# A written-out step order exchanged for another one, in an RWKV-6 plus HyperMixer kernel on one core

## The chip, the core and the metric

The kernel runs on one NeuronCore of a Trainium2 chip. The metric is the device time of one execution in microseconds (µs). Three runs of the kernel before took 100.81, 100.89 and 101.01 µs; the median is 100.89 µs.

The profile names the engines PE (matrix multiplies), PEld (the loading of the stationary operand, which overlaps PE), DVE (vector engine), ACT (scalar engine), POOL (GpSimd) and SP, which only issues transfers here. "SPq", "ACTq" and "PEq" are the instruction sequencers of these engines.

## The reference

Inputs are `r, k, v, w` of shape (4 batches, 8 heads, 768 positions, 48), `u` of shape (8, 48) and three small weight matrices. What is computed, cut to its core:

```python
for t in range(S):                       # attention with a decaying state
    y[:, :, t] = r_t · (state + outer(u * k_t, v_t))
    state      = w_t[..., None] * state + outer(k_t, v_t)
x     = y with the heads side by side    # (4, 768, 384)
W_tok = (x @ w_q) (x @ w_k)^T / 8        # a 768 x 768 mixing matrix for each batch
out   = relu(W_tok @ x) @ w_out          # (4, 768, 384), float32
```

## The kernel before, in words

**Tiling.** The 768 positions of a batch are cut into three units of 256 positions; there are 12 units, numbered 0 to 11, so that units 2, 5, 8 and 11 end a batch. A unit is two chunks of 128 positions. Inside a chunk the recurrence is written as matrix products, and a 48 x 48 state per head goes from chunk to chunk.

**Steps.** A unit is a chain of steps with short names, which all texts here use. A number behind a name is the unit (`cw.2` belongs to unit 2), a second one the chunk.
- Loads: `wg`, `kg`, `rg`, `vg` bring a unit's w, k, r and v, 384 KB each, all issued by SP.
- `ln` (ACT, L615) takes the logarithm of w; `cw` (PE) sums it along the positions; `ep` and `en` (ACT, L675 to L686) exponentiate the sums.
- `k16`, `r16`, `v16` (POOL, ACT or DVE, L627 and L800) cast the loads to bf16; `kT`, `rT` (PE) transpose; `vp` (PE) reorders v, and `VB` (ACT or DVE) copies it out of PSUM.
- `ks`, `qT`, `RT` (DVE, some `ks` on ACT) and `KT` (POOL or DVE, L773) make the scaled operands; `A` (PE) multiplies them, `AM` (DVE, L860) masks the product.
- `dps`, `dd`, `Vd` make the diagonal term with `u`; `kb`, `kd`, `sn` (PE), `SB` (DVE, L929) make the new state; `ya`, `yi` (PE) and `X` (DVE, L972) the output y.
- `xt`, `XT`, `wk`, `wq`, `QK` transpose y and project it. At the end of a batch follow `T`, `TS`, `mx`, `rl` (relu, into tile MX), `fp`, `os` and the store `st`.
- `wcast` (POOL, L560 to L562) casts the weights, which the loads `wts` and `wtso` bring. Thirty steps `z` are multiplications of a zero tile that keep PE warm; each one can be issued or left out.

**What sets the order.** Nothing is scheduled at run time. Every engine executes its own list of instructions in the order of the program, and the steps' order in that list is written out by hand-off tables: `RANK` (L243) gives each of 787 steps its place on its engine, `ALT` (L280) says for each step with a choice which way it is done. The letters A, D and P in `ALT` are engines; E and e are two ways of doing a PE step, which use the PE array whole, or in halves by rows, by columns or both (the plan calls these modes 0 to 3, and counts `SWITCH` = 93 ns when the mode changes; f is a third way). E of a `z` step issues it, e leaves it out.

`Plan.order` (L104 to L238) then walks the five lists with a model of time of its own, to fix in which sequence the instructions are written down and which PSUM bank each buffer gets. Its constants stand in L38 to L46: durations, the delay until a result is seen by another engine (`AFTER`), a model of the load queue, and one of the fetching of PE's own instructions: after every `BLOCK` = 128 matmuls, the first time after `FIRST` = 94, the plan lets PE wait until a fetch is done. The time that the plan computes is not carried into the program; only order, ways and banks are.

**Buffers.** Each load has a ring of four buffers (`RINGS`, L361), so a load of unit n waits for the cast of unit n - 4. PSUM has 8 banks, which the plan hands out.

Of the kernel before, what the change touches and what calls it, by code (L numbers as in the profile page):

```python
# [33 lines left out]
class Plan:  # L34
# [1 line left out]


    SWITCH = 93  # L38
    LAND = 1950
    COLD = 5200  # L40
    BLOCK, FIRST = 128, 94
    FETCH = (4700, 3700, 74000)
    DEEP = dict(Q=1850, R=2700, T=1850)
    ASIDE, BLOCKED = 1200, 980
    OVER = dict(A=100, D=80, P=42)
    AFTER = dict(E=200, A=80, D=62, P=65, S=80)  # L46

# [56 lines left out]
    def order(self):  # L104
# [5 lines left out]
        wires = {}  # L110
        for s in self.steps:
            if s["eng"] in "QL":
                wires.setdefault(s["after"][0]["i"], s)
        free = dict.fromkeys("EADPSQRT", 0)
        place = dict.fromkeys("EADPS", 0)
        rings = {k: [] for k in self.rings}
        owners, done, mode, moving = [None] * 8, [], 0, []
        count, edge, ready = 0, self.FIRST, 0
        used = [{} for _ in range(8)]

        def banks(s):
            b = s["banked"]
            if b is None or b.kind == "s" or s["part"] is None:
                return [] if b is None else range(b.bank, b.bank + 1 + (b.kind == "w"))
            return [b.bank + s["part"]]
# [34 lines left out]
                    t = max(t, clear(ring[-size]))  # L160
            return t, None

        def run(s, t, took):
            s["start"], s["end"] = t, t + took + s["lag"]
            free[s["eng"]] = t + took
            done.append(s)
            for x in banks(s):
                used[x][s["eng"]] = s["end"]

        while True:  # L170
            heads = [(start(q[place[e]]), e) for e, q in queues.items() if place[e] < len(q)]
# [4 lines left out]
            s = queues[e][place[e]]  # L176
# [10 lines left out]
            took = s["dur"] + self.SWITCH * change  # L187
            if e == "E" and t < self.COLD and s["fn"] is not None:
                took = took * 8 // 5
            n = s["opts"][s["way"]][5]  # L190
            if n:
                first = count
                count += n
                while count > edge:
                    cross = t + took * (edge - first) // n
                    if cross < ready:
                        took += ready - cross
                        cross = ready
                    ready = cross + self.FETCH[cross >= self.FETCH[2]]
                    held = cross + self.ASIDE  # L200
                    for i, (m, x) in enumerate(moving):
                        if x > held:
                            moving[i][1] = x = x + self.BLOCKED
                            m["end"] = max(m["end"], x)
                            x = wires[m["i"]]
                            x["start"], x["end"] = m["end"], m["end"] + x["dur"]
                    free["R"] = max(free["R"], held) + self.BLOCKED
                    edge += self.BLOCK
            lock = s["lock"] and e == "D"
            if lock:  # L210
                took += max(0, free["P"] - t)
            if s["i"] in wires:
                m = wires[s["i"]]
                x = t + took
                full = [0]
                *durs, deep = m["wires"][s["way"]]
                lanes = [(q, d) for q, d in zip("QRT", durs) if d]
                for q, d in lanes:
                    free[q] = max(free[q], x)
                    full.append(free[q] + deep * d // max(durs[0], 1) - self.DEEP[q])  # L220
                    free[q] += d
                m["start"] = x
                m["end"] = max([x] + [free[q] for q, _ in lanes])
                moving = moving[-3:] + [[m, free["R"]]]
                took = max(took, max(full) - t)
                for q, d in lanes:
                    free[q] = max(free[q], t + took)
                    m["end"] = max(m["end"], t + took)
            run(s, t, took)
            if lock:  # L230
                free["P"] = max(free["P"], t + took)
            if s["i"] in wires:
                done.append(m)
                x = wires[m["i"]]
                x["start"], x["end"] = m["end"], m["end"] + x["dur"]
                done.append(x)
        assert len(done) == len(self.steps)
        return done  # L238

RANK = [  # L243
# [35 lines left out]
]  # L279
ALT = ("DDEDAEAEADPEEEAEDEeEeeAEDPPEDPAeAeDPEefDeEEEEAeAPPEADPeAEAPEeEAEEEeAeDAEAEAeAEAEAEAPAEAD"  # L280
       "PeAEAPEEfAEEEEEAeAAPEDPPeAEAPeEfAEeEEeDEAAPeDPPeDeAPEEEAeEEEDeAAEAEAEAeAEAEAPPEDPPEAEAPE"
       "EfAeeEEeAEDPAEAPPeDEAPEEEAeEEEeDEAPPEDPPeAeDPEeEAEEEEDeAAEAEAeAeAeAEAAPEAPPeAEAPeEEAeEEE"
       "eAeDPPEAPAeAEAPEEEAEEEEeAeAPPEEeDPeAeAPPEEEAEEEeAEDDfDEDADEDeDeeADEAeAeeADeDeAeeDDEeeeEE"
       "eeeEEEeEeeeEeeeEeEeeeEee")

WARM = 30

# [2 lines left out]
def kernel(  # L290
# [13 lines left out]
    B, H, S, D = r.shape  # L304
# [19 lines left out]
    R = C // 2  # L324
# [217 lines left out]
    def weights():  # L542
# [8 lines left out]
        def f_o(e):  # L551
            cuts = (0, C) if e == "S" else (0, FEW, C)
            for p0, p1 in zip(cuts, cuts[1:]):
                nc.sync.dma_start(out=view(wo_f, 0, [[DM, NK], [1, DM]], p0=p0, pn=p1 - p0),
                                  in_=moe_w_out.rearrange("(n p) d -> p n d", p=128)[ds(p0, p1 - p0)])
        l = [plan.dma(("wts",), 1000, 1200, f, deep=1200)[1],
             plan.dma(("wtso",), 500, 1500, f_o, deep=500)[1]]

        def cast(e):
            nc.gpsimd.tensor_scalar_mul(wq_sb, wq_f, scale)  # L560
# [622 lines left out]
```

## Time and profile before

| what | value |
|---|---|
| runs | 100.81, 100.89, 101.01 µs |
| span of the profiled execution (first to last instruction) | 102.1 µs, so 1.2 µs over the median of the runs |
| PE busy | 90.8 µs, 2123 matmuls and as many weight loads |
| DVE, ACT, POOL busy | 82.5, 78.2, 63.0 µs |
| moved by DMA | 24.70 MB, mean 242 GB/s |
| mean granted PE clock | 0.996 of full speed |

The profile has a page for the whole execution and answers questions on it. In its timeline a row gives the start in µs from the first instruction, the time taken, engine, line, operation, the tiles written and read, their shapes, and in brackets how long the engine stood idle before and what ended that. A row "by stretches" gives start and end of a stretch, its length, the busy time of each engine in it with the number of its instructions, the granted clock, the busy share of the DMA engines and the rate in GB/s. A matmul's end is modelled: the matmuls overlap, so the distance from one start to the next says what a step costs.

### The profile page before, as it was taken

Reading aid. Unit: us, or ns where it says so; the run is one execution under the profiler, and the core shown is the slowest. Engines: PE = TensorE matmul, PEld = TensorE weight load, DVE = VectorE, ACT = ScalarE, POOL = GpSimd, SP = SyncE. Lnnn points to the kernel's source line nnn. Section 1 sums busy time; section 2 is a strip of 40 time slices with the busy share of each in tenths; the row PEclk is TensorE's granted clock in tenths of the full one; section 3 lists DMA queues with packets and bytes.
Section 4 is the critical chain, followed back from the end, with each engine's and each line's share of the span. In section 5 each row is a group of like instructions: output and inputs, shape, how many; then the busy total and the mean of one; then the engine's idle time right before and its main releaser. Section 6 shows DMA issues by size and latency. Waiting matters only on the chain.

```text
span 102.1 us, 4927 instructions
## 1 busy us (share of the span) xinstructions
PE 90.8 (89%) x2123; PEld 67.8 (66%) x2123; DVE 82.5 (81%) x154; ACT 78.2 (77%) x137; POOL 63.0 (62%) x76
## 2 busy tenths in 40 slices
PE   5998689997999699899999897979998999999950
PEld 2353456975778596786987885657786869775520
DVE  6319979999999789999998696969898599753560
ACT  5349981999779768799999899795987897558710
POOL 4478687393688947988989859696499304100000
PEclk9999999999999999999999999999999999999998
DMA  1999999999899999999997699910993009140783
GB/s 39 310 323 351 328 332 301 283 317 286 242 325 337 325 257 287 312 307 307 302 281 209 193 277 330 281 37 39 277 336 136 0 37 396 43 157 24 306 310 140
DMA packets 43078, 24.70 MB, mean 242 GB/s; under 512 B 30512, under 2 KB 41904, under 8 KB 43056
## 3 DMA queue, kind: packets, MB, share of 16 engines
q1 hardware_dynamic: 42896, 24.19, 79.5%
q8 instruction: 16, 0.26, 1.0%
q10 hardware_dynamic: 160, 0.20, 0.6%
q14 instruction: 6, 0.05, 0.2%
HBM read 19.66 MB, written 4.72 MB: 239 GB/s over the span
## 4 chain that ended last, share of the span: by engine, by line
PE 64%; DVE 13%; SPq 5%; DMA 5%; issue 5%; POOL 3%; ACT 1%; DVEq 1%; POOLq 0%
PE PS L335 64%; DMA rg<-in_r_dram 5%; DVE AM L860 4%; SPq L395 4%; DVE X L972 4%; POOL KT L773 2%; SPq L401 1%; DVE RT L755 1%; DVE os L521 1%; POOL r L627 1%; DVE SB L929 1%; DVE KT L773 1%; DVE ks L521 1%; DVE qT L744 1%; ACT os L519 0%
## 5 line engine op out<-in xcount | busy, mean ns | idle before, releaser
L860 DVE TENSOR_TENSOR AM<-PS,US 128x1024 bf16<-128x1024 f32 x24 | 29.1, 1216 | 1.8 <-PE PS L335 1.4
L773 POOL TENSOR_TENSOR KT<-ks,en 128x1024 bf16<-128x1024 bf16 x8 | 17.1, 2132 | 8.4 <-DVE ks L521 3.4
L839 POOL TENSOR_TENSOR Vd<-VB,dd 128x768 bf16<-128x768 bf16 (+1 forms) x13 | 17.2, 1328 | 7.3 <-ACT dd L519 5.5
L675 ACT ACTIVATE ep<-PS 128x512 bf16<-128x512 f32 x20 | 11.0, 607 | 4.5 <-PE PS L335 4.5
L335 PE MATMUL PS<-wo,MX 128*64 128x384 bf16 (+1 forms) x102 | 13.8, 328 | 0.0
L972 DVE TENSOR_TENSOR X<-PS,Vd 128x768 bf16<-128x768 f32 (+1 forms) x13 | 11.6, 890 | 2.4 <-PE PS L335 1.9
L335 PEld LDWEIGHTS <-KT 64*128 64x128 bf16 (+3 forms) x360 | 10.1, 97 | 4.6 <-issue 1.9
L686 ACT ACTIVATE en<-PS 128x1024 bf16<-128x1024 f32 (+1 forms) x14 | 12.6, 905 | 0.1
L615 ACT ACTIVATE lw<-wg 128x768 bf16<-128x768 f32 x12 | 10.2, 858 | 2.6 <-DMA wg<-in_w_dram 2.6
L525 ACT ACTIVATE MX<-PS 128x768 bf16<-128x768 f32 (+1 forms) x12 | 8.8, 732 | 2.9 <-PE PS L335 2.8
L519 ACT COPY os<-PS 128x768 f32<-128x768 f32 (+1 forms) x11 | 8.2, 746 | 2.6 <-PE PS L335 2.5
L335 PE MATMUL PS<-RT,KT 64*128 64x128 bf16 (+1 forms) x232 | 9.6, 218 | 0.4 <-ACT XT L517 0.2
L335 PE MATMUL PS<-Z 128*128 128x512 bf16 (+2 forms) x26 | 8.9, 457 | 1.1 <-DVE Z L418 1.0
L335 PE MATMUL PS<-VB,AM 128*128 128x48 bf16 (+1 forms) x200 | 8.2, 184 | 1.3 <-issue 1.3
L335 PEld LDWEIGHTS <-MX 128*64 128x64 bf16 (+1 forms) x102 | 6.8, 104 | 3.6 <-DVE MX L527 0.5
L800 POOL CAST v<-vg 128x768 bf16<-128x768 f32 x9 | 7.5, 828 | 1.9 <-DMA vg<-in_v_dram 1.9
L519 ACT CAST VB<-PS 128x768 bf16<-128x768 f32 x10 | 8.1, 806 | 0.4 <-PE PS L335 0.2
L755 DVE TENSOR_TENSOR RT<-PS,ep 128x512 bf16<-128x512 bf16 x20 | 8.0, 412 | 0.4 <-ACT MX L525 0.4
L744 DVE TENSOR_TENSOR qT<-PS,ks 128x1024 bf16<-128x1024 bf16 x12 | 8.1, 678 | 0.0
L335 PE MATMUL PS<-ID,r 128*128 128x128 bf16 (+1 forms) x120 | 7.2, 213 | 0.9 <-POOL r L627 0.5
L335 PEld LDWEIGHTS <-AM 128*128 128x128 bf16 (+1 forms) x200 | 6.4, 97 | 2.3 <-issue 1.7
L335 PE MATMUL PS<-CM,lw 64*128 64x128 bf16 (+1 forms) x208 | 7.7, 217 | 0.0
(95 smaller groups left out, 195.9 us busy)
## 6 DMA issues: line engine op xcount, KB each, us to landing
wg<-in_w_dram SPq DMA_DIRECT2D x12, 384.0 KB, 5.6
kg<-in_k_dram SPq DMA_DIRECT2D x12, 384.0 KB, 5.3
rg<-in_r_dram SPq DMA_DIRECT2D x12, 384.0 KB, 5.7
vg<-in_v_dram SPq DMA_DIRECT2D x12, 384.0 KB, 6.1
out_dram<-os SPq DMA_DIRECT2D x9, 384.0 KB, 2.9
out_dram<-os SPq DMA_DIRECT2D x5, 192.0 KB, 1.9
wof<-in_moe_w_out_dram SPq DMA_DIRECT2D x1, 576.0 KB
out_dram<-os ACTq DMA_DIRECT2D x1, 192.0 KB
```

Of the source, the lines that this page charges most:

```text
L335: return nc.tensor.matmul(o, l, rr, start=start, stop=stop, skip_group_check=True, is_transpose=trans)
L519: nc.scalar.copy(o, i)
L525: nc.scalar.activation(o, i, ACT.Relu)
L615: nc.scalar.activation(view(lw.tile, 0, [[64, H], [512, 2], [1, D]]), view(g["wg"].tile, 0, [[D2, H], [D, 2], [1, D]]), ACT.Ln, bias=0.0, ...
L675: nc.scalar.activation(view(ep.tile, to, [[EW, 8], [step, 2], [1, Q]]), view(at(cw), x, [[C, 8], [Q, 2], [1, Q]]), ACT.Exp, bias=LIFT, sca ...
L686: nc.scalar.activation(en.tile[:, ds(cs[0] * 512, w_)], at(cw)[:, ds(cs[0] * 512, w_)], ACT.Exp, bias=-LIFT, scale=-1.0)
L744: lambda e: nc.vector.tensor_tensor(plain(qT), turned(second), plain(ks), ALU.mult),
L755: nc.vector.tensor_tensor(view(RT.tile, c * 512, [[256, 2], [Q, 8], [1, Q]]), view(at(kr, BF16), second + c * 256, [[apart, 2], [Q, 8], [1 ...
L773: x.tensor_tensor(KT.tile[:, w], ks.tile[:, w], en.tile[:, w], ALU.mult)
L839: (nc.vector if e == "D" else nc.gpsimd).tensor_tensor(Vd.tile[:, cols], VB.tile[:, cols], view(dd.tile, cs[0] * H, [[1, len(cs) * H], [0, ...
L860: AMs[c] = add(("AM", n, c), {"D": 1221}, lambda e, c=c, A=A: nc.vector.tensor_tensor(view(AM[c].tile, 0, [[C, 8], [1, C]]), view(at(A), 0 ...
L972: lambda e, c0=c0, nc_=nc_: nc.vector.tensor_tensor(view(X.tile, (2 * i + c0) * DM, [[D2, NP * nc_], [D, 2], [1, D]]), view(at(y), c0 * NP ...
```

## The change

No operation of the computation is added or removed. The constants of the plan's model and its treatment of transfers and of instruction fetches are other ones; a transfer now waits in one model queue, a fetch waits for half of what stands before it in that queue and pushes the transfers behind it; and `RANK` and `ALT` are exchanged for tables that were found with that model.

```diff
     SWITCH = 93
-    LAND = 1950
     COLD = 5200
     BLOCK, FIRST = 128, 94
-    FETCH = (4700, 3700, 74000)
-    DEEP = dict(Q=1850, R=2700, T=1850)
-    ASIDE, BLOCKED = 1200, 980
+    ASKED, FETCH, READY = 560, 1000, 1400
+    ARRIVE, AHEAD, LAND, FREE, OPEN = 700, 2600, 450, 220, 2600
+    PATIENT, SLOW = 1300, 1.02
...
-                    ready = cross + self.FETCH[cross >= self.FETCH[2]]
-                    held = cross + self.ASIDE
...
+                    asked = cross + self.ASKED
+                    behind = max(0, free["R"] - asked)
+                    wait = min(behind, (behind + self.PATIENT) // 2)
+                    begin = asked + wait
+                    over = now = begin + self.FETCH
+                    ready = over + self.READY
...
 RANK = [
...
 ALT = (...
...
-             plan.dma(("wtso",), 500, 1500, f_o, deep=500)[1]]
+             plan.dma(("wtso",), 500, 1800, f_o, deep=500)[1]]
```

Read off the tables, the lists differ as follows. Places in the list of SP count from 0.

| list | before | after |
|---|---|---|
| SP, places 3 to 20 | vg.0 wg.1 kg.1 rg.1 vg.1 wg.2 kg.2 rg.2 wg.3 kg.3 rg.3 vg.2 vg.3 wtso wts wg.4 kg.4 rg.4 | rg.1 wg.1 kg.1 vg.0 kg.2 kg.3 vg.1 wg.2 vg.2 rg.2 kg.4 wg.3 rg.3 vg.3 wg.4 wts wtso rg.4 |
| SP, first store | st.2.0 at place 48, among the last loads | st.0.0 at place 38, ahead of 12 loads; then st.2.0 and st.3.0 among the last ones |
| ACT, from `ks.1` on | (another order) | ks.1 ep.1 VB.0 k16.2 VB.1 kd.1 ln.2 v16.2 en.2 ep.2 ln.3 VB.2 en.3 ks.3 ep.3 |
| POOL, from `r16.2` on | r16.2 Vd.1 k16.3 v16.2 v16.3 wcast Vd.2 r16.4 Vd.3 KT.4 | r16.2 k16.4 KT.2 r16.3 v16.3 KT.3 Vd.2 wcast r16.4 KT.4 |
| `KT` | POOL for units 1 and 4 to 10, DVE for 2 and 3 | POOL for units 2 to 10, DVE for 1 |
| PE matmuls | 2123 | 2059 |
| changes of mode along PE's list | 117 | 106 |
| PE, last batch | T.11 fp.7 mx.9 mx.10 fp.8 mx.9 (chunk 1) | fp.7 and fp.8 ahead of T.11; T.11 wq.11 mx.9 mx.10 |

The engines' counts of steps stay near each other: PE 267 and 267, ACT 127 and 124, DVE 138 and 138, POOL 56 and 59.

More of the change, by code (lines that the diff above doesn't have):

```diff
@@ L113, in order @@
                 wires.setdefault(s["after"][0]["i"], s)
-        free = dict.fromkeys("EADPSQRT", 0)
+        free = dict(E=0, A=0, D=0, P=0, S=self.FREE, Q=self.OPEN, R=self.OPEN)
         place = dict.fromkeys("EADPS", 0)
@@ L161, in start, with landed @@
             return t, None
[L163 to L168, printed above, removed]
+        def landed(m):
+            x = wires[m["i"]]
+            x["start"], x["end"] = m["end"], m["end"] + self.LAND
         while True:
@@ L198, in order @@
                         cross = ready
-                    ready = cross + self.FETCH[cross >= self.FETCH[2]]
-                    held = cross + self.ASIDE
[L201 to L207, printed above, removed]
+                    asked = cross + self.ASKED
[4 more added lines that the diff above has]
+                    ready = over + self.READY
+                    for x in moving:
+                        m, b, d = x
+                        if b >= begin - self.PATIENT // 2:
+                            x[1] = max(now, b)
+                            now = x[1] + d
+                            m["end"] = max(m["end"], now)
+                            landed(m)
+                            free["R"] = max(free["R"], now)
+                    free["R"] = max(free["R"], over)
                     edge += self.BLOCK
@@ L213, in order @@
                 m = wires[s["i"]]
[L214 to L229, printed above, removed]
+                d = m["wires"][s["way"]][0]
+                x = t + took + self.ARRIVE
+                q, r = max(free["Q"], x), max(free["R"], x)
+                free["Q"], free["R"] = q + d, r + int(d * self.SLOW)
+                took = max(took, max(q, r) - self.AHEAD - t)
+                m["start"], m["end"] = min(q, r), max(free["Q"], free["R"])
+                moving = moving[-8:] + [[m, r, free["R"] - r]]
+            s["start"], s["end"] = t, t + took + s["lag"]
+            free[e] = t + took
+            done.append(s)
+            for x in banks(s):
+                used[x][e] = s["end"]
             if lock:
@@ L233, in order @@
                 done.append(m)
-                x = wires[m["i"]]
-                x["start"], x["end"] = m["end"], m["end"] + x["dur"]
-                done.append(x)
+                landed(m)
+                done.append(wires[m["i"]])
         assert len(done) == len(self.steps)
@@ L243 @@
 RANK = [
[35 rows of a table removed]
-]
[L280 to L284, printed above, removed]
[35 rows of a table added]
+]
+ALT = ("DDEAPEAEDPDeEEDeDeeEEEDeAAPeADPEAEDPEEfAeEEEEAeDAPeDPAEAEAPEEEDeEEEAeAAEAEAEAEAEAEAPPEAP"
+       "PeAEAPEEfAeEEEEDeAPPEAPAeAEDPEEfDeeEEEAeAAPEAPPeAEDPEEEDEEEeAeDAEAeAEAeAeAEAAPEDPPeAEAPe"
+       "EfAeEEEEDeDPPEAPPeAEAPEEEAEeEEEDeAPPEAPPeAEAPEEEAeEEfAEAAEAeAeAEDEAeAPPEAPPeAEAPeEEDEEEE"
+       "eDEAPPEDPPeAEDPeEEAEEEEeAeAPPEEEDPeAeDPPeEEAEEEEDEDAEAEAADEAeDEEAAeDeAEEDAeAeDEEDDeeeeeE"
+       "eeeeeeEeEeeeeeeEEEEEEeee")
 WARM = 30
```

70 rows, old and new, of the table RANK are left out of this document.

## The prediction, made before the result was known

> **What bounds the kernel now.** I read the page first, then the table by stretches, then PE's waits, and only then single rows of the timeline.
>
> ```profile
> span 102.1 us, 4927 instructions
> ...
> PE 90.8 (89%) x2123; PEld 67.8 (66%) x2123; DVE 82.5 (81%) x154; ACT 78.2 (77%) x137; POOL 63.0 (62%) x76
> ...
> q8 instruction: 16, 0.26, 1.0%
> ```
>
> ```profile
> 20.00:28.00 8.00, 7.25 (x179) 5.80 (x177) 8.00 (x13) 7.23 (x13) 5.33 (x7) 1.00 1.02 283
> ...
> 36.00:56.00 20.00, 19.72 (x502) 16.08 (x502) 19.19 (x30) 18.21 (x33) 16.95 (x15) 1.00 1.00 284
> 56.00:78.00 22.00, 19.79 (x524) 15.57 (x516) 19.10 (x30) 18.56 (x33) 17.09 (x14) 1.00 0.75 219
> ```
>
> Columns are stretch, length, then PE, PEld, DVE, ACT and POOL. From 36 µs on PE is the bound: 19.7 of 20 µs busy, with DVE and ACT close behind. Before that the loads (DMA share 1.0) and, from 20 to 28, DVE (8.00 of 8.00) hold it back. From 56 to 78 PE idles 2.2 µs although nobody else is full. What it waits for:
>
> ```profile
> PE PS L335 <- issue: 3.0, 5, 1.0
> ```
>
> ```profile
> 0.00:29.46 29.46, 25.46 (x477) 1.00 1.00 286
> ...
> 0.00:35.56 35.56, 30.56 (x606) 1.00 1.01 293
> 35.56:56.51 20.95, 20.32 (x512) 1.00 0.98 279
> 56.51:62.16 5.65, 4.90 (x128) 1.00 0.92 263
> 62.16:67.75 5.59, 4.74 (x128) 1.00 0.86 237
> 67.75:77.95 10.20, 9.94 (x256) 1.00 0.63 194
> ```
>
> "Issue" is no semaphore. I cut the span at the ends of these five idle times: 606 matmuls are 94 + 4 x 128, and every further piece holds a whole number of 128. A matmul comes with one weight load, so 128 matmuls are 256 instructions, and 2123 of them make 16 such blocks; the page counts 16 instruction transfers of 16 KB. PE stops where a block of its own program has not come. These five stops cost 3.0 µs. The transfer starts late:
>
> ```profile
> q8 instruction: 1, 0.02, 5.0%
> ```
>
> This is the transfer table for 32.8 to 34.2 µs; PE had entered a new block at 29.46 (the 478th matmul, 94 + 3 x 128) and went on into the next one at 35.57. So in the loaded stretch it takes 6.1, 5.65 and 5.59 µs from entering one block until the next is ready (29.46, 56.51, 62.16). The last stop ends at 77.95; after it, with the loads gone, there is none.
>
> [...]
>
> **The change, term one: PE's own work.** There are 2059 matmuls instead of 2123, and 106 changes of mode instead of 117. A change costs 0.10 µs by the distances between starts:
>
> ```profile
> 38.35 0.40 PE L335 MATMUL PS<-RT,KT 64*128 64x128 bf16 x8
> 38.69 0.36 PE L335 MATMUL PS<-v,PM 64*64 64x384 bf16 x4
> ...
> 41.17 0.40 PE L335 MATMUL PS<-RT,KT 64*128 64x128 bf16 x8 [0.21 <-POOL KT L773]
> 41.41 0.26 PE L335 MATMUL PS<-ID,KT 48*128 48x48 bf16 x8
> ```
>
> (0.34 with a change, 0.24 without.) Eleven fewer give -1.1. Against that, four or five `xt` are done whole instead of in halves:
>
> ```profile
> 25.05 0.35 PE L335 MATMUL PS<-ID,X 64*128 64x64 bf16 x12
> 25.31 0.40 PE L335 MATMUL PS<-RT,KT 64*128 64x128 bf16 x8
> ...
> 27.14 0.50 PE L335 MATMUL PS<-ID,X 128*128 128x128 bf16 x6
> 27.48 0.34 PE L335 MATMUL PS<-UB,qT 128*128 128x2 bf16 x8
> ```
>
> That is 0.34 against 0.26, together +0.4; `vp`, `rT` and `ya` changes add about 0.2. **Term one: -0.5 µs**, bounds -1.1 and 0. Summing every step's distance in this manner, the old list holds 81.4 µs of work without the `z` steps, the new one 80.9; "work" below is this sum up to a step.
>
> **Term two: the stops.** Between block entries the old list has, from the fourth on, 4.7, 5.1, 4.1, 4.7, 6.0, 4.7, 4.6, 4.9, 5.0 µs of work; the new one 5.1, 5.7, 5.3, 5.9, 3.7, 5.2, 5.5, 4.7, 4.2. Against 5.6 to 6.1 until ready, the longer pieces lose less. The short one, 3.7, lies where `st.0.0` stands in SP's list: SP waits there for `os.0`, loads behind it wait too, and the transfer of instructions should meet an empty queue. I take 0.4 for the first piece, 0.5 for the sixth, 0.3 for the rest: 1.2 instead of 3.0. **Term two: -1.8 µs**, bounds -2.8 (only 0.2 left) and +1.0 (6.1 - 5.1, 6.1 - 3.7 and 5.6 - 5.2 all fall due).
>
> **Term three: the front.** Loads arrive in SP's order. Their places and first uses, where the user waited for them:
>
> ```profile
> 4.22 0.84 ACT L615 ACTIVATE lw<-wg 128x768 bf16<-128x768 f32 x1 [2.15 <-DMA wg<-in_w_dram]
> ...
> 11.72 0.83 POOL L627 CAST r<-rg 128x768 bf16<-128x768 f32 x1 [0.31 <-DMA rg<-in_r_dram]
> ...
> 14.16 0.84 ACT L615 ACTIVATE lw<-wg 128x768 bf16<-128x768 f32 x1 [0.45 <-DMA wg<-in_w_dram]
> ...
> 17.65 0.83 POOL L627 CAST r<-rg 128x768 bf16<-128x768 f32 x1 [0.31 <-DMA rg<-in_r_dram]
> ...
> 24.59 0.83 POOL L800 CAST v<-vg 128x768 bf16<-128x768 f32 x1 [1.52 <-DMA vg<-in_v_dram]
> ```
>
> These are places 0, 6, 8, 10 and 15, so a place costs (24.59 - 4.22) / 15 = 1.36 µs. Now `vg.1` moves from place 7 to 9: 16.4. Behind it hang `v16.1` (0.83), `vp.1`, `VB.1` and `kd.1`, and on ACT `ln.2` is queued behind these two.
>
> ```profile
> 13.16 2.13 POOL L773 TENSOR_TENSOR KT<-ks,en 128x1024 bf16<-128x1024 bf16 x1 [0.61 <-DVE ks L521]
> 14.96 0.80 ACT L519 CAST VB<-PS 128x768 bf16<-128x768 f32 x1
> 17.12 0.59 PE L335 MATMUL PS<-CM,lw 64*128 64x128 bf16 x10
> 22.48 1.12 DVE L773 TENSOR_TENSOR KT<-ks,en 128x1024 bf16<-128x1024 bf16 x1
> 25.32 0.68 DVE L773 TENSOR_TENSOR KT<-ks,en 128x1024 bf16<-128x1024 bf16 x1
> 27.45 1.15 POOL L562 CAST wo<-wof 128x1152 bf16<-128x1152 f32 x1
> ```
>
> 16.4 + 0.83 is 17.3; `vp.1` and its way to ACT take 0.5, `VB.1` 0.80, `kd.1` 0.5, `ln.2` 0.84: `cw.2` starts at 20.0 instead of 17.12. The new list does 1.0 µs more work ahead of it, so it is 1.6 behind there. `wg.3` at place 14 comes at 23.2, `cw.3` at 24.1. On POOL follow `KT.2`, `r16.3`, `v16.3` (`vg.3`, place 16, 25.9) and `KT.3`, until 26.7 + 2.13 = 28.8, and PE has `kb.3` behind that; `cw.4` starts at 29.7 with 16.6 of work done, which the old list had done at 28.75. The unit's later loads come earlier than before, and `wcast`, `r16.4` and `KT.4` (2.2 + 0.83 + 2.13 after `Vd.2`) keep up with PE by my count. In return DVE, full from 20 to 28, loses the two `KT` rows, 1.8 µs. **Term three: +0.95**, bounds 0 (DVE's gain pays) and +1.6 (nothing is caught up).
>
> **Term four: the end.** `mx.9` needs `TS.11`, which needs the last `T.11`:
>
> ```profile
> 91.28 0.37 PE L335 MATMUL PS<-X,QK 128*64 128x384 bf16 x2
> ...
> 91.44 1.18 PE L335 MATMUL PS<-wo,MX 128*64 128x384 bf16 x12
> 91.68 0.56 DVE L521 CAST TS<-PS 128x384 bf16<-128x384 f32 x1
> ...
> 92.55 0.36 PEld L335 LDWEIGHTS <-TS 64*128 64x128 bf16 x12 [0.30 <-DVE TS L521]
> ```
>
> From the last `T` to `mx.9` are 1.27 µs, which `fp.7` (91.44) fills. The new list has `fp.7` and `fp.8` earlier, as cover for other waits there, and only 0.46 of work in the hole: 0.8 lost, some 0.3 won elsewhere. **Term four: +0.5**, bounds 0 and +0.8. The output's last steps and stores stay.
>
> The sum is -0.5 - 1.8 + 0.95 + 0.5 = -0.85 on a span of 102.1, so 101.2. The median of the runs lies 1.2 below that span; the forecast for the runs is 100.89 - 0.85, **100.0 µs**.
>
> **Rivals.**
> - *The front costs nothing and the stops go.* For it: DVE, not the loads, was full from 20 to 28. Against it: ACT's queue behind `VB.1`. Terms -0.5, -2.6, +0.2, +0.3: 98.3.
> - *The stop moves to the short block (slower).* If `st.0.0` does not stop the loads while the ninth block is fetched, or its own 384 KB stand before the fetch, the block takes 5.6 to 6.1 against 3.7 of work. It decides from about 4.0 on; the price is 2.0: 102.0. For it: the old list had its worst delays exactly between 50 and 68 µs.
> - *The stops do not come from late instructions*, so all 3.0 stay: -0.5 + 0.95 + 0.5 gives 101.8. Against it: the multiples of 128. [...]
> - *Nothing to measure:* the stops are as long as before at other places, and front and end are covered: about 100.8.
>
> **How the numbers follow.** Forecast 0.45, its own range 99.3 to 100.7; first rival 0.22; the slower one 0.20; late instructions not the cause 0.06; no difference 0.07. A measurement of this kernel tells about 0.2% (0.2 µs) from no change. The forecast's range lies faster for nine tenths of it: faster 0.62, same 0.11, slower 0.27. The range goes from the first rival's 98.3 to the slower one's 102.0.
>
> **What would show it.** Right: PE's "issue" waits near 1.2 µs, none of more than 0.5 between 53 and 58; 2059 matmuls; `cw.2` near 20 and PE idle some 1.8 µs between 15 and 18; `cw.4` near 29.7; an idle 0.8 ahead of `mx.9`. Wrong: issue waits of 3 µs or more, a stop of 2 µs at the ninth block, `cw.4` before 28.8, or a new wait of PE for DVE or POOL between 36 and 78, where I took the old 1.2 µs of other waits unchanged.

## The result, and the profile after

The new lists made the kernel slower. Their runs took 103.85 to 104.97 µs, median 104.64, against a median of 100.95 of the kernel before beside them: a ratio of 1.0325, 95% interval 1.0223 to 1.0428. Two later comparisons, on chips 11 and 5, gave 1.0249 (1.0163 to 1.0336) and 1.0347 (1.024 to 1.0453). Some executions of a kernel are a few per cent slower than the rest (105.49 µs beside 100.81 to 101.01 of the kernel before); the ratios here and below, as recorded, leave those out and are not the quotients of the medians, which are taken over all runs. The forecast was 100.0, the range ended at 102.0.

First the page of the kernel after: span, busy times, the DMA queue of instructions, the chain that ended last, and the group of POOL's casts of v.

```profile
span 103.3 us, 4796 instructions
...
PE 90.5 (88%) x2059; PEld 67.3 (65%) x2059; DVE 80.5 (78%) x154; ACT 78.3 (76%) x134; POOL 67.3 (65%) x79
...
q8 instruction: 16, 0.26, 1.1%
...
PE 28%; DMA 27%; POOL 14%; issue 9%; DVE 8%; SPq 6%; ACT 4%; POOLq 0%; DVEq 0%; ACTq 0%
...
L795 POOL CAST v<-vg 128x768 bf16<-128x768 f32 x10 | 8.3, 826 | 9.2 <-DMA vg<-in_v_dram 8.8
```

The same two rows in the profile before:

```profile
PE 64%; DVE 13%; SPq 5%; DMA 5%; issue 5%; POOL 3%; ACT 1%; DVEq 1%; POOLq 0%
...
L800 POOL CAST v<-vg 128x768 bf16<-128x768 f32 x9 | 7.5, 828 | 1.9 <-DMA vg<-in_v_dram 1.9
```

PE's busy time hardly moved (90.8 before), the span grew by 1.2 µs. Over a quarter of the chain is now transfers, and POOL stood idle 8.8 µs for loads of v instead of 1.9. The stretch from 15 to 20 µs before, and then this one and the prediction's stretches after, in the same columns (PE, PEld, DVE, ACT, POOL, granted clock, DMA share, GB/s):

```profile
15.00:20.00 5.00, 4.79 (x124) 3.81 (x124) 5.00 (x12) 2.80 (x7) 2.73 (x4) 1.00 1.02 292
```

```profile
15.00:20.00 5.00, 2.82 (x54) 1.78 (x54) 2.49 (x7) 2.24 (x4) 3.66 (x4) 0.83 0.89 234
20.00:28.00 8.00, 7.27 (x175) 6.03 (x168) 6.85 (x13) 6.37 (x10) 6.72 (x7) 0.89 1.01 274
36.00:56.00 20.00, 19.45 (x457) 15.67 (x456) 18.50 (x33) 18.52 (x31) 16.64 (x15) 1.00 0.89 255
56.00:78.00 22.00, 21.11 (x556) 17.04 (x550) 19.17 (x30) 18.93 (x34) 20.34 (x18) 1.00 0.86 250
```

From 56 to 78 PE is 1.3 µs busier than before, 21.11 against 19.79: the stops are gone. (In the execution of experiment 1 the old lists reach 21.05 there too.) But from 15 to 20 it is busy for 2.82 of 5 µs, and DVE, the bound there before, for 2.49. PE's waits after, summed by what ended them:

```profile
PE PS L330 <- POOL v L795: 2.1, 2, 1.9
...
PE PS L330 <- DVE AM L855: 0.7, 2, 0.5
PE PS L330 <- DVE qT L739: 0.7, 2, 0.5
PE PS L330 <- POOL k L622: 0.6, 1, 0.6
PE PS L330 <- DVE TS L516: 0.6, 1, 0.6
...
PE PS L330 <- ACT VB L514: 0.4, 1, 0.4
```

There is no "issue" among them: none of the 3.0 µs of late instructions is left. The longest wait is a new one, 1.9 for v. Single rows of the timeline after:

```profile
16.34 0.83 POOL L795 CAST v<-vg 128x768 bf16<-128x768 f32 x1 [3.90 <-DMA vg<-in_v_dram]
...
17.22 0.50 PE L330 MATMUL PS<-v,PM 64*128 64x384 bf16 x4 [1.94 <-POOL v L795]
...
19.74 0.64 PE L330 MATMUL PS<-CM,lw 64*64 64x128 bf16 x16 [0.24 <-ACT lw L610]
...
30.54 0.61 PE L330 MATMUL PS<-CM,lw 64*128 64x128 bf16 x16
...
43.49 0.20 PE L330 MATMUL PS<-ID,KT 48*128 48x48 bf16 x2 [0.43 <-ACT VB L514]
...
66.31 0.40 PE L330 MATMUL PS<-ID,k 128*128 128x128 bf16 x4 [0.61 <-POOL k L622]
...
94.57 0.29 PE L330 MATMUL PS<-QK,TS 64*128 64x64 bf16 x4 [0.56 <-DVE TS L516]
```

They are `vg.1`'s cast, `vp.1`, `cw.2` (predicted at 20.0), `cw.4` (29.7), two new waits in the middle, and `mx.9`.

### The profile page after: what moved, and what is told of

It reads as the page before. It is cut to its first block, busy times and chain, and to the rows that moved or that the text cites. A ratio compares the mean times of both kernels' runs of the same rounds, so it can differ in the third digit from the quotient of the medians.

```text
span 103.3 us, 4796 instructions
## 1 busy us (share of the span) xinstructions
PE 90.5 (88%) x2059; PEld 67.3 (65%) x2059; DVE 80.5 (78%) x154; ACT 78.3 (76%) x134; POOL 67.3 (65%) x79
## 4 chain that ended last, share of the span: by engine, by line
PE 28%; DMA 27%; POOL 14%; issue 9%; DVE 8%; SPq 6%; ACT 4%; POOLq 0%; DVEq 0%; ACTq 0%
PE PS L330 28%; DMA vg<-in_v_dram 16%; DMA rg<-in_r_dram 11%; POOL KT L768 4%; POOL Vd L834 4%; SPq L390 3%; SPq L396 3%; POOL v L795 2%; DVE AM L855 2%; POOL r L622 2%; DVE X L967 2%; POOL k L622 2%; DVE RT L750 1%; ACT os L514 1%; DVE qT L739 1%
## 5 line engine op out<-in xcount | busy, mean ns | idle before, releaser
L768 POOL TENSOR_TENSOR KT<-ks,en 128x1024 bf16<-128x1024 bf16 x9 | 19.2, 2130 | 1.8 <-ACT ks L512 1.7
L795 POOL CAST v<-vg 128x768 bf16<-128x768 f32 x10 | 8.3, 826 | 9.2 <-DMA vg<-in_v_dram 8.8
L330 PE MATMUL PS<-wo,MX 128*128 128x384 bf16 (+1 forms) x96 | 13.8, 327 | 0.0
L514 ACT CAST VB<-PS 128x768 bf16<-128x768 f32 x12 | 9.6, 798 | 3.7 <-PE PS L330 3.3
L330 PEld LDWEIGHTS <-KT 64*128 64x128 bf16 (+4 forms) x368 | 10.1, 98 | 3.2 <-issue 1.7
L622 POOL CAST r<-rg 128x768 bf16<-128x768 f32 x10 | 8.5, 852 | 2.1 <-DMA rg<-in_r_dram 2.0
L924 DVE SCALAR_TENSOR_TENSOR SB<-PS,ep 128x192 bf16<-128x192 f32 x20 | 7.0, 350 | 3.0 <-PE PS L330 2.9
L330 PEld LDWEIGHTS <-MX 128*128 128x128 bf16 (+1 forms) x96 | 6.4, 103 | 4.1 <-DVE MX L522 0.5
L330 PE MATMUL PS<-ID,k 128*128 128x128 bf16 (+1 forms) x104 | 7.6, 222 | 1.5 <-POOL k L622 0.6
L330 PE MATMUL PS<-VB,AM 128*128 128x48 bf16 x192 | 7.7, 184 | 0.5 <-DVE AM L855 0.5
```

What stands on the lines that cost most here:

```text
L330: return nc.tensor.matmul(o, l, rr, start=start, stop=stop, skip_group_check=True, is_transpose=trans)
L514: nc.scalar.copy(o, i)
L622: op(view(o.tile, 0, [[64, 4], [256, 4], [1, D]]), view(g[src].tile, 0, [[4 * D, 4], [D, 4], [1, D]]))
L768: x.tensor_tensor(KT.tile[:, w], ks.tile[:, w], en.tile[:, w], ALU.mult)
L795: v16s = add(("v16", n), {"P": 826, "A": 810}, lambda e: (nc.scalar.copy if e == "A" else nc.gpsimd.tensor_copy)(view(v16.tile, 0, [[D, H] ...
```

## The experiments

Times of the kernel before wandered from chip to chip (medians 100.7 to 102.2 µs in the comparisons below), so ratios are compared, not times.

**1. The kernel before once more (no edit).**

> The kernel before, unchanged, to see which of its executions the prediction's profile was. In the changed kernel every execution takes 1.7 us more than its own span (104.97 and 103.3; 103.85 and 102.1). If that holds here too, the profile of before that the prediction used (span 102.1) belongs to an execution of about 103.8 us, and the runs of 100.9 have spans of about 99.2. Theory A, an untypical sample: spans near 99.2, and a profile with clearly less than the 3.0 us of stops by late instructions. Theory B, a typical sample: span near 102.1, time near 100.9, five stops with 3.0 us.

Ratio 1.0037 (0.9969 to 1.0104), as it must be. Its profiled execution took 101.82 µs. The head of its page, and then the first of PE's waits:

```profile
span 100.1 us, 4927 instructions
```

```profile
PE PS L335 <- issue: 1.2, 2, 0.7
```

A third stop of 0.15 brings it to 1.4 µs. The execution that the prediction was built on had 3.0 µs of stops in a span of 102.1. In every profiled execution of this study whose time is known it is the span plus 1.7 to 1.8 µs (103.3 and 104.97 after, 100.1 and 101.82 here). By that the one of the prediction took about 103.8, some 3 above the runs that were shown with it: it was no usual execution.

**2. More warming steps in the hole ahead of `vp.1`, and `vg.1` two places earlier.** The granted clock after was half from 18.35 on:

```profile
18.35:21.76 3.41, 3.17 (x59) 2.31 (x59) 2.11 (x4) 2.90 (x5) 2.89 (x3) 0.50 1.09 329
```

```diff
+for z in (0, 1, 2, 3, 4, 6, 7, 8):     # a_warm: eight more z steps ahead of vp.1
+    RANK[757 + z] = 33
+    ALT = ALT[:346 + z] + "E" + ALT[347 + z:]
```

```diff
+for i, place in {89: 7, 134: 8, 131: 9, 206: 10}.items():   # a_vg1: vg.1, kg.2, wg.2, kg.3
+    RANK[i] = place
```

> The changed kernel with eight more multiplications of the zero tile put where PE idles 1.94 us ahead of vp.1; nothing else moves. Theory clock: the idle time halves PE's clock from 18.35 to 21.76 us, which costs up to 1.7 us of PE's work; with the eight the granted clock stays 1.00 between 17 and 25 us and the time falls by 0.7 to 1.7 us. Theory loads: what counts is that vg.1, wg.2 and what hangs behind them come late; the clock recovers but PE waits for data instead, and the time falls by less than 0.4 us.

> The changed kernel with four loads in another order on SP: vg.1 at place 7 and wg.2 at place 9, kg.2 at 8 and kg.3 at 10 (they stood at 9, 10, 7 and 8). Theory loads: vp.1 starts near 14.9 instead of 17.2, cw.2 near 18.3 instead of 19.7, the clock stays at 1.00, and the time falls by 1.5 to 3 us. Theory lists: the rest of the lists, not these loads, makes the kernel slower; the idle time goes, but the time falls by less than 0.7 us.

With the zero steps the clock stayed whole in the front (mean granted clock of the span 0.995, against 0.983 after), and the ratio was 1.0272 (1.0161 to 1.0383): among the three of the new lists. So the halved clock is not what makes them slower; a share of it below the interval, about 1 µs, is not excluded. With `vg.1` at place 7 the ratio was 1.0169 (1.0071 to 1.0267), perhaps a part back. In its profile `vp.1` started at 15.38 and `cw.2` at 17.95, 1.8 earlier than after, and then PE waited again (this execution took 105.59 µs, the other three 103.03 to 104.14, so the waits show where the time can go, not how much usually does):

```profile
20.90 0.23 PE L332 MATMUL PS<-ID,r 128*128 128x128 bf16 x1 [1.43 <-POOL r L624]
...
24.71 0.29 PE L332 MATMUL PS<-CM,lw 64*128 64x128 bf16 x4 [1.64 <-ACT VB L516]
```

The idle time went to `rT.2`, whose cast now stood on POOL behind that of the later `kg.3`, and to `cw.3`.

**3. Old and new lists joined at 36 µs, and the old lists in the new plan.** `hb36` has the old places and ways for each step that the old plan starts before 36 µs and the new ones for the rest; `ha36` the reverse; both use the new plan's code. `b_plan` has the old tables whole, in the new plan's code: engines execute the same lists as before, and only the PSUM banks differ (129 of the 204 choices of a bank). `a_again` is the new kernel unchanged.

```diff
 class Plan:                  # b_plan: the code of after
 ...
-RANK = [ 0, 0, 0, 0, 8, 1, ...
+RANK = [ 0, 0, 0, 0, 1, 2, ...   # the tables of before, ALT too
```

> The changed kernel, unchanged, beside the others of this set, because the time of the kernel before moves between 100.6 and 103.6 us from execution to execution. Both theories: 2 to 3 us over the kernel before; no stop by late instructions, PE's clock halved once between 18 and 22 us.

> Each engine's list follows the old table for the steps that the old plan starts within its first 36 us (92 of PE, 54 of DVE, 41 of ACT, 26 of POOL, 28 of SP) and the new table for all others; the plan's code is the new one. Theory front: by 35 us the new lists are 2.7 us behind at equal work and nothing of it comes back, so this kernel is 2 to 3 us faster than the changed one and at or below the kernel before, by up to 1 us, as the stops are rarer. Theory rest: the second part of the new lists is what costs; then it stays within 1 us of the changed kernel.

> The reverse: the new table for the steps that the new plan starts within its first 36 us, the old table for all others. Theory front: the 2.7 us of the front stay and the old stops come on top, so it is no faster than the changed kernel (103.5 to 106 us). Theory rest: it comes back to within 1 us of the kernel before.

> The old tables with the new plan's code: every engine's list stays, only PSUM banks and the sequence in which the lists are written down can differ. Theory lists: same as the kernel before within 0.5 us. Theory banks: another choice of banks makes PE or DVE wait for a bank, and it is slower by 1 us or more.

`hb36` gave 1.048 (1.0418 to 1.0543) and `ha36` 1.0619 (1.0522 to 1.0715), both slower than either parent and outside what either theory expected. They tell nothing of front against rest; that each part meets banks and buffers which the other half did not leave as it expects is a guess that no run tests. `b_plan` is the surprise: 1.0198 (1.0128 to 1.0268), 2 µs for banks alone. Its new waits:

```profile
24.78 0.20 PE L330 MATMUL PS<-ID,KT 48*128 48x48 bf16 x2 [0.62 <-DVE X L967]
...
51.19 0.22 PE L330 MATMUL PS<-ID,k 128*128 128x128 bf16 x1 [0.47 <-DVE AM L855]
62.55 0.22 PE L330 MATMUL PS<-SB,RT 48*128 48x48 bf16 x4 [0.56 <-DVE qT L739]
85.66 0.21 PE L330 MATMUL PS<-SB,RT 48*128 48x48 bf16 x3 [0.51 <-ACT MX L520]
```

None of them stands in the profile of experiment 1. At 51.19, for example, `kT.7` needs `k16.7`, a cast of POOL, but PE was released by DVE's `AM.6.1`, the reader of the bank that `kT.7` fills; in the other three, too, PE was released by the reader of what the bank held before. Together they are 2.2 µs. That this is also the size of the loss is partly chance: the profile of `b_plan` has no stop for late instructions, where that of experiment 1 has 1.4 µs.

**4. The loads given a start.** In both kernels, with their own lists and their own banks (written into the plan as numbers), the first casts wait until the load at place 9 has landed; nothing else is changed.

```diff
+for key in (("ln", 0), ("k16", 0, 0), ("k16", 0, 1)):
+    s = the step with this key
+    s["after"].append(the landing of vg.1 (after) or kg.2 (before))
+    ...                      # its engine first copies one element of that load
```

> The kernel before, with its own lists and its own PSUM banks written down as numbers, but the first casts (ln.0, k16.0) wait on all engines until the load at place 9 of SP's list has landed (by copying one element of it first), so that the loads have a start of some 12 us (16.4 instead of 4.2). The time grows by those 12 us less what the loads had cost the front. What counts is the distance to the new lists treated in the same manner: see there. Alone: between 105 (the front had lost 8 us to loads) and 112 (it had lost next to nothing).

> The new lists with the banks of the new plan, and the same start for the loads (place 9 there is vg.1). Theory loads (the loss of the new lists is made in the front, by steps that wait for a load that comes late, and by DVE having less to do meanwhile): with the start the front no longer waits, so the distance to the old lists with the same start falls from +2.5 to +3.3 us to within 0.5 of zero: no stops (-1.4 against a usual execution), less work (-0.5), +0.6 at mx.9 and +1.3 of new waits between 36 and 90 stay. Theory lists' own order (the new order of DVE's, ACT's and POOL's work costs time whatever the loads do): the distance stays at 2 us or more.

Old lists 113.51 µs, 1.13 times before (1.1137 to 1.1463); new lists 112.7, 1.1201 (1.1118 to 1.1284). What was +2.5 to +3.5% is now -0.8 µs, at most +1.5 by the ends of the two intervals. The -0.8 flatters the new lists: their first casts were let go 0.8 µs earlier (the first row of the table below). From 1 to 79 µs of work they need 86.87 µs with the start against 86.28 of the old lists, 0.6 more, where without it they needed 1.9 and 3.1 more. POOL's casts of v with the start, in the new lists:

```profile
L799 POOL CAST v<-vg 128x768 bf16<-128x768 f32 x10 | 8.1, 824 | 3.1 <-DMA vg<-in_v_dram 3.0
```

3.0 µs of waiting instead of 8.8. In the measure of the prediction (the time at which PE starts the step that has the same sum of work ahead of it, in one profiled execution each):

| work done | old lists (`b_again`) | new (`a_again`) | new (first profile) | old with start | new with start |
|---|---|---|---|---|---|
| 1 µs | 7.13 | 7.29 | 7.33 | 18.99 | 18.16 |
| 22 µs | 35.16 | 36.81 | 37.19 | 47.00 | 46.41 |
| 79 µs | 93.97 | 96.05 | 97.28 | 105.27 | 105.03 |

From 1 to 22 µs of work the old lists need 28.0 µs with and without the start: loads cost them nothing. The new ones need 29.5 and 29.9 without it and 28.25 with it. That is 1.3 to 1.6 µs of loads. (The clock does not explain it: with the start it was half until 20.25 in the old lists and until 21.76 in the new ones, with a mean of 0.954 and 0.937 over the span.) After it, from 22 to 79, the new lists lose 0.4 (with the start too) to 1.3 µs more.

**5. The new lists in the old plan's code.**

```diff
 class Plan:                  # the code of before
 ...
-RANK = [ 0, 0, 0, 0, 1, 2, ...
+RANK = [ 0, 0, 0, 0, 8, 1, ...   # the tables of after, ALT too
```

> The new lists with the old plan's code, so that only the PSUM banks are chosen otherwise (by the old plan's times). Theory banks belong to the list and to the plan that made it: slower than the new lists with the new plan by 1 to 3 us, as the old lists became slower by 2.1 with the new plan's banks; PE gets new waits for the engine that still reads a bank. Theory the new plan's model chooses worse banks for any list: it becomes faster than the new lists with the new plan, by 1 to 2 us. No difference: within 0.5 us of it.

1.0486 (1.0403 to 1.057), some 2 µs over the new lists in their own plan. So the new plan does not choose worse banks as such; in both directions tried, a list did badly with banks that were not made with it.

**6. Lists judged by both plans.** Small moves in the tables were kept where they lowered the mean end of the plan in both models, with drawn delays of single steps. The edit is the tables alone (29 of 376 letters of `ALT` in the old lists, 37 in the new ones).

```diff
-RANK = [ ...
+RANK = [ ...                 # other places, ALT too
```

> The old lists, improved by small moves (a step a few places along its engine's list, or done the other way) that were kept where they lowered the mean end of the plan as both models see it, the old one and the new one, each undisturbed and with three sets of drawn delays of single steps; banks as the old plan chooses them. By that mean it gains 1.8 us (old model +0.2, new model -2.2 undisturbed). Theory a list looks good in the model that it was chosen with: what is judged by two models and by delays keeps a part of its gain, so 0.3 to 1.5 us faster than before. Theory the models miss what costs here (loads and casts in the front): no faster, within 0.5 us or slower.

> The new lists, improved in the same manner by the mean of both models; banks as the new plan chooses them. By that mean it gains 1.4 us (old model -2.6, new model +1.2 undisturbed). Theory a list looks good in the model that it was chosen with: 0.5 to 2 us faster than the new lists, which stood 2.5 and 3.2% above before, so a ratio to before of 1.01 to 1.025. Theory the models miss what costs here: 1.025 or more.

`b_both` gave 0.9999 (0.9954 to 1.0044): none of the 1.8 µs. `a_both` gave 1.0221 (1.0136 to 1.0305), inside the range of its first theory, but its interval reaches into the second's; it is hardly better than the new lists, and still stops where they stop (one of its six runs took 147.87 µs, for a reason that is not known):

```profile
17.69 0.35 PE L327 MATMUL PS<-v,PM 64*64 64x384 bf16 x2 [2.10 <-POOL v L792]
```

So neither list shows the gain that the models see. Walking each plan's own code over each table, with the banks fixed as the kernel had them, gives the plan's end; beside it the measured distance to before:

| kernel | old plan's end, µs against before | new plan's end, µs against before | measured |
|---|---|---|---|
| new lists | +5.0 | -4.1 | +2.5 to +3.5% |
| `a_oldplan` | +5.8 | -0.4 | +4.9% |
| `b_plan` | +2.3 | +0.2 | +2.0% |
| `b_both` | +0.2 | -2.2 | 0.0% |
| `a_both` | +2.3 | -2.8 | +2.2% |
| `b_vg1` (below) | +4.2 | +0.7 | +4.8% |

The old plan has the sign right wherever a difference was measured; the new one calls four of them faster, none of which is. One place where it errs is in the traces: the new plan lets PE's first instruction block be fetched at 14.2 µs, behind `vg.1`, which lands at 14.99. On the chip it moved at 13.08. The transfer table after for 13.0 to 14.3 µs has it, beside a full DMA (share 1.15):

```profile
q8 instruction: 1, 0.02, 5.6%
...
vg<-in_v_dram SPq DMA_DIRECT2D x1, 384.0 KB, 6.6
```

`vg.1`, issued at 9.04 and so before PE entered a new block (10.1, its 95th matmul), which the plan takes as the cause of the fetch, landed at 16.29, 1.3 after the plan's time. That the fetch alone makes up these 1.3 µs was not tested.

**7. That load alone.** In `b_vg1` the old lists and banks get one thing of the change, `vg.1` at place 9. In `a_swap` the new ones lose one thing, `vg.1` and `kg.3` exchanged. `a_third` is the new kernel unchanged.

```diff
+for i_, x_ in {131: 7, 134: 8, 89: 9}.items():     # b_vg1: wg.2, kg.2, vg.1
+    RANK[i_] = x_
```

```diff
+RANK[206], RANK[89] = RANK[89], RANK[206]          # a_swap
```

> The old lists and the old banks, with one thing of the change alone: vg.1 goes from place 7 of SP's list to place 9 (wg.2 and kg.2 one place forward). In the profile of the new lists the first fetch of PE's instructions moved at 13.08 us, after kg.2, and vg.1, which had been issued before it was asked for, landed at 16.29, while the new plan had it at 14.99. Theory the front is lost by vg.1 behind that fetch: PE stops ahead of vp.1 for 1.3 to 2 us, vp.1 starts near 17.0 instead of 14.4, and 1.5 to 3 us of it stay to the end (the old plan's own model says +4.2, the new one's +0.7). Theory the place of vg.1 is a small part: within 0.7 us of before.

> The new lists and the new banks, with vg.1 and kg.3 exchanged in SP's list (places 9 and 8), nothing else. Theory vg.1 behind the fetch: vg.1 lands near 15.0 instead of 16.1 to 16.3, vp.1 and cw.2 start 1.0 to 1.3 us earlier, and 0.4 to 1.2 us stay at the end (rg.2 and wg.3, which land no earlier, take part of it back). Theory small part: the end moves by less than 0.3 us. The models give +2.9 (new) and +0.2 (old) for it.

> The new lists unchanged, beside the two others on the same chip: 1.025 to 1.033 times before, and vg.1 landing at 16.1 to 16.3.

`b_vg1`: 1.0484 (1.0366 to 1.0603), 106.42 µs against 101.81.

```profile
16.43 0.83 ACT L804 CAST v<-vg 128x768 bf16<-128x768 f32 x1 [3.49 <-DMA vg<-in_v_dram]
17.17 0.84 ACT L619 ACTIVATE lw<-wg 128x768 bf16<-128x768 f32 x1
17.31 0.54 PE L339 MATMUL PS<-v,PM 64*64 64x384 bf16 x4 [3.09 <-ACT v L804]
```

One load two places later stops PE for 3.09 µs, and its cast stands ahead of `ln.2` on ACT. The loss, 4.6 µs by the medians, is more than the upper end of what was expected. A part of it can be the clock, which was half from 15.62 to 22.45, while PE had work without a break:

```profile
17.30:22.45 5.15, 5.14 (x71) 3.49 (x70) 2.94 (x5) 1.73 (x4) 2.74 (x3) 0.50 1.08 320
```

How much is the stop and how much the clock was not separated. `a_swap`: 1.0315 (1.0212 to 1.0418), 104.43 µs against 104.71 for `a_third` (1.0347, a little above the 1.025 to 1.033 expected). Here the small-part theory was right, as far as such intervals tell. `vg.1`'s wait is gone, and three others are there:

```profile
18.49 0.31 PE L333 MATMUL PS<-CM,lw 64*64 64x128 bf16 x8 [1.00 <-ACT lw L613]
...
20.73 0.23 PE L333 MATMUL PS<-ID,r 128*128 128x128 bf16 x1 [0.72 <-POOL r L625]
...
24.20 0.29 PE L333 MATMUL PS<-CM,lw 64*128 64x128 bf16 x4 [1.30 <-ACT lw L613]
```

These are `cw.2`, `rT.2` and `cw.3`, behind `wg.2`, `rg.2` and `wg.3`. In the new lists `kg.2`, `kg.3` and `kg.4` are loaded at places 7, 8 and 13 instead of 9, 12 and 19, and `vg.2` at 11 instead of 14; `vg.1`, `wg.2` and `rg.2` come two places later for it, `wg.3` three. In the two cases tried (`a_vg1`, `a_swap`) moving one of them back uncovered the next.

## Why the prediction was wrong

**The base.** The sum was made against an execution with a span of 102.1 and then carried to the median by "the median of the runs lies 1.2 below that span". A time below its own span cannot be: it is 1.7 above it. This was the warning that the profiled execution had lost some 3 µs that the median had not, and half of that (3.0 against 1.4 in another execution) was the very term that the change was to win back. Nor does a measurement here tell 0.2% from no change, as the prediction took from three runs: the intervals are about 1% to either side.

**Term two, the stops (-1.8, bounds -2.8 to +1.0).** The stops did go: six profiles of the new lists and their variants show none (four) or up to 0.5 µs (two) of "issue", the short ninth block did no harm, and nothing of the slower rival came. But the term was mis-sized: against the execution of experiment 1 there were 1.4 µs to be won, not 3.0. And that longer pieces of work are the reason is not shown: with the old list of PE, and so the same pieces, `b_plan` has no such stop and the execution of experiment 1 has 1.4 µs of them, so other waits in a piece, or the execution, decide as well.

**Term three, the front (+0.95, bounds 0 to +1.6): the step that failed first.** Its beginning was right to 0.3 µs: `vp.1` waits 1.94 for v, `cw.2` starts at 19.74 (predicted 20.0). What failed is "The unit's later loads come earlier than before ... keep up with PE by my count", with DVE's gain. `cw.4` came at 30.54 instead of 29.7, 1.8 behind the old 28.75 and so above the upper bound, and at 22 µs of work the new lists lay 2.0 behind (1.65 in `a_again`). The bound itself was too low: by the prediction's own figures `cw.2` is 20.0 - 17.12 - 1.0 = 1.9 behind, not 1.6. DVE's two rows fewer showed no gain: DVE was busy for 2.49 of the 5 µs from 15 to 20 (it waited 2.11 µs in one piece for PE, which waited for that load), and was the one to wait for afterwards (0.53 ahead of `ya.2.1`, at 32.29). Experiment 4 shows that it is the loads: with a start for them the loss of the front falls from 1.5 and 1.8 µs, against the old lists, to 0.24 (one profiled execution each). Experiment 7 shows that it is not `vg.1` alone.

**Term four, the end (+0.5, bounds 0 to +0.8).** Near: 0.56 idle ahead of `mx.9`, where 0.8 was forecast; the 0.3 "won elsewhere" was not measured.

**Term one (-0.5).** 2059 matmuls, as counted; the term was not measured by itself.

**What had no term.** The "old 1.2 of other waits unchanged" between 36 and 78. The 1.2 was misread: of PE's waits there in the profile before, 2.0 are "issue" and 0.4 the others. The new profile has 0.43 at 43.49, 0.61 at 66.31 and 0.24 at 69.52, and 0.18 at 82.51, 1.5 together, against 0.4 in the execution of experiment 1. A new wait of PE for POOL (66.31) was one of the prediction's own signs of being wrong. The bank choice was named in the change and priced nowhere, while `b_plan` and `a_oldplan` show that it can cost 2 µs. Which share of these mid waits is due to banks was not separated: at 43.49 `kb.5` needs POOL's `KT.5` and was released by ACT's `VB`, the reader of `vp.5`, which held one of its banks before; at 66.31 it is the late cast itself.

**The sum by what was measured**, the first profile after against the execution of experiment 1: front +2.0 (a stop of 0.53 that the old lists have there is taken off in it), the other stops -0.9, mid waits +1.0, end +0.6, work -0.5 (as forecast, not measured), together +2.2; the spans differ by 3.2. The 1.0 left is hardly idle time: from 22 to 79 µs of work the waits under 0.15 µs add up to 0.16 after and 0.07 before. There PE counts as busy for 57.91 µs against 57.43 with the same sum of work; why, and where the rest is, stays open. Spans of later executions of the new lists (101.8 and 102.3) lie nearer, but the chips differ: before's median was 102.2 on the one of experiment 1 and 100.7 on that of `a_again`, so such a difference of two spans is uncertain by about 1.5 µs, and only the ratios are not.

## What to carry to other kernels

Before taking a term from a profile, see whether its execution is a usual one: compare its time, not its span, with the runs, and where the thing to be won varies from execution to execution, take it from a usual one. Where loads fill the DMA queue, write down for each load its place before and after and its first user: a load that moves up for a later unit pushes others back (here `vg.1` by two places: `vp.1` started at 17.22 instead of 14.29). In `b_vg1` one stop of PE of 3.09 µs, with the halved clock around it, went with a loss of 4.6 µs. A list found with a model can fit that model alone: here the model that the new lists did not come from had the sign right. Keep the buffers' places together with the list they were made for.

## What the runs showed of the hardware

- The transfer of a PE instruction block (at 13.08 µs) moved ahead of a 384 KB load whose issue began at 9.04, a µs before PE entered a new block (10.1); the load landed at 16.29. The transfer took about 1.2 µs of DMA engine time (5.6% of 16 engines over 1.3 µs). What such a fetch costs the loads behind it was not measured by itself.
- How long PE stops for its own instructions changes between executions of one program, 3.0 and 1.4 µs, and between programs with the same list of PE: none in `b_plan`.
- Ahead of the last steps the granted clock was halved for 3.41 µs after (18.35 to 21.76), 6.83 in `b_vg1` (15.62 to 22.45), 10.24 in `b_head` (until 20.25) and 13.65 in `a_head` (until 21.76): one to four times 3.41. The mean over the span was 0.983, 0.966, 0.954 and 0.937. In `a_again`, where PE waited 1.3 µs for v, the mean was 1.000, in `a_oldplan` (1.4) 0.999, in `a_third` (1.7) 0.981, in `a_both` (2.1) 0.976. PE's busy time, the granted clock, the DMA share and GB/s in three pieces of 3.41 to 3.42 µs:

```profile
14.93:18.35 3.42, 1.48 (x32) 1.00 0.85 200
...
16.44:19.86 3.42, 1.98 (x38) 1.00 0.87 257
...
21.69:25.10 3.41, 2.05 (x62) 1.00 1.10 320
```

The first is after, followed by half a clock (18.35 to 21.76: 0.50), the second `a_third`, the same (21 to 23: 0.50). The third is `a_swap`, whose mean clock was 0.991; 3.41 µs at half a clock would alone have left 0.983. What makes the clock fall, and from which idle time on, these runs do not show.
